# Moving slab transposes into the last stage, and opening the O*wo stage with the heads of wo that are there

## The chip, the cores and the metric

The kernel runs on one core of a Trainium2 chip. The metric is the time of one execution on the device, in microseconds (us). The core has five engines that run their own instruction streams: TensorE (PE, matrix products; its weight loads are shown as PEld), VectorE (DVE), ScalarE (ACT), GpSimd (POOL) and SyncE (SP). Here POOL and SP mostly issue DMAs: POOL plain copies, SP transposing ones. Each engine works in its own order and waits for the others by semaphores.

## The reference

The kernel computes a forward pass and its gradients. With x of 2048 x 576, 32 heads of width 128, keys and values given, and F = 4608:

```python
xn = layernorm(x)
q = heads(xn @ wq)
p = softmax(q @ k^T * Dh ** -0.5)
o = p @ v                      # rows of 32 * 128 columns
s = o @ wo
g = silu((sigmoid(xn @ w_gate) * (xn @ w_up)) @ w_down)
out = x + s * g
```

The outputs are `out` and the gradients of x, the keys, the values, wq, wo, w_gate, w_up and w_down for a given gradient of `out`. All arrays are bf16.

## The kernel before

The work runs in six stages, one after the other. Rows come in 16 tiles of 128 (NT = 16).

1. Layer norm, gate and up products; the activations go to DRAM.
2. The product with w_down, and everything that follows from it by rows. `g2_d` and `dsg_d` in DRAM keep the factors for the later O*wo stage.
3. Attention, one head after the other, forward and backward. Each head leaves its output columns in `on2_d`, its query gradient in `dq2_d` and two slabs in `kvT_d`: its key and value gradients, each 128 x 2048, still transposed. The stage exists twice in the program, as `attention(True)` and `attention(False)`; a flag computed on the device chooses one, and a branch leads around the other.
4. The O*wo stage (from L910): for each row tile, 32 heads x 2 products of `o` with wo (512 and 64 columns) into two accumulators, then ACT and DVE make `out` and the gradient `doB` of the inner product, which PE also transposes.
5. The gradients of the gated unit (b1, from L1034), 18 blocks of 256 columns.
6. The gradients of wo and wq (dwo and dwq, from L1126), 32 heads x 2 products, and last (from L1159) the gradient of x, in 8 pairs of row tiles. In the tables below these two parts are listed apart: the dwo and dwq stage and the last stage.

The parts that matter for the change:

**wo in old buffers.** wo is not given memory of its own. `wo_parts` places its 32 heads in buffers that attention stops using: heads 0 to 16 in `dsT` (dead 0), 17 to 19 in an old key buffer (dead 1), 20 to 22 in `Vn` (dead 2), 23 to 25 in `dOn` (dead 3) and 26 to 31 in the end of `xnT` (dead 4). While the last head is worked on, `paced` (L838) issues the loads, at most two heads each: a one-element POOL copy that waits for a slab of probabilities, then the DMA on POOL.

**The transposed output.** The O*wo stage needs each row tile of `on2_d` transposed: 128 x 4096, by one transposing DMA on SP (`load_oT`, L585). Three buffers `oTs` take turns: the memory of `KQ`, the end of `xnT`, and `xn_all`. Tiles 0 and 1 are loaded inside attention, tile 2 at the start of the O*wo stage, each later one when the tile three before it has been multiplied.

**Orders.** In stages 4 to 6 SP and POOL follow the order of the program text (`manual_schedule`), while the other engines are scheduled by dependences. In attention all are.

**Slabs.** The 64 slabs of `kvT_d` have to be turned (2048 rows of 128) and written to the outputs of the keys and values. `kv_turn` (L1018) issues the transposing DMA on SP into a tile `kvn` of two buffers; `kv_store` (L1025) issues the store on POOL, which waits for the transpose. Stage b1 does two of them for each of its 18 blocks. The dwo and dwq stage does one for each head until none is left.

**dwo and dwq.** For each head, `accumulate` (L978) runs 16 row tiles x 2 matmuls into one of four pairs of accumulators, and ACT copies the result out: to `dwo` (two buffers; stored by POOL, L1143) and to `dqT` (two buffers; turned by SP, L1145). Every eight heads POOL loads two blocks of 2 MB for the next eight (L1010, L1013). SP also loads w_up and w_gate transposed (L63).

**The last stage.** `seq` lists 80 chunks: for each pair of row tiles six chunks of 12 x 256 x 128 (from `du_d` and `dg_d`) and four of 8 x 256 x 128 (from `dq2_d`); the first two pairs are interleaved, so that their query chunks are numbers 12 to 19. SP loads each transposed (`load_chunk`, L1119) into one of four buffers (`ah`, `cf`), and PE multiplies it (L1188). SP loads wq transposed among chunks 3 to 11. When a pair is complete, `finish` (L1193) runs a chain on ACT and DVE and POOL stores two row tiles (L1218).

Of the kernel before, what the change touches and what calls it, by code (L numbers as in the profile page):

```python
# [13 lines left out]
P = 128  # L14
# [52 lines left out]
def kernel(  # L67
# [517 lines left out]
    def load_oT(dst, st):  # L585
        nc.sync.dma_start_transpose(dst, on2_d[st * P:(st + 1) * P, :])
# [8 lines left out]
    def attention(fast):  # L595
        with ExitStack() as es:
# [169 lines left out]
            def put(slot, cols, fn):  # L766
                units.setdefault(slot, []).append((cols, fn))
# [73 lines left out]
                load_wo_rows(view, view_h0[id(view)], a, b)  # L841
            view_h0 = {}
            for view, h0, n, dead in sorted(wo_parts, key=lambda w: dead_from[w[3]]):
                view_h0[id(view)] = h0
                for k in range(0, n, 2):
                    at = min([f for f in free if f >= dead_from[dead]] or [NT - 1])
                    if at in free:
                        free.remove(at)
                    put(bl + at, 0, lambda at=at, view=view, k=k, n=n: paced(at, view, k, min(k + 2, n)))
            for st in range(min(2, NT)):  # L850
                put(bl + NT + skew * st, 0, lambda st=st: load_oT(oTs[st], st))
            slot = 0
            while slot < 2 * NT * H or units:
                us = units.pop(slot, [])
# [19 lines left out]
    def late(name, bufs=1, **kw):  # L874
        return tc.tile_pool(name=name, bufs=bufs, reuse_waits="tile", **kw)
# [9 lines left out]
    with late("pc") as pc, late("pcw") as pcw, late("pcf") as pcf, \  # L885
# [22 lines left out]
                    nc.gpsimd.memset(wdT_sb[:LO, i, r0:r0 + WCH], 0.0)  # L908

        with late("c1l3", 4) as ldp3, late("c1s", 2) as sb, \  # L910
                late("c1ps", 2, space=PSUM) as ps, late("c1pt", 2, space=PSUM) as pst:
            wo_of = {}
            for view, h0, n, _ in wo_parts:
                for k in range(n):
                    wo_of[h0 + k] = view[:, k, :]
            oTs.append(oT_view(xn_all[:].rearrange("p t d -> p (t d)"), 0))
            if NT > 2:
                load_oT(oTs[2], 2)
            SG1 = 1
            NG1 = NT // SG1  # L920

            def group_loads(g):
                res = []
                for nm, src in (("dsg", dsg_d), ("g2b", g2_d), ("xb", x2)):
                    t_ = ldp3.tile([P, SG1, D], bf, name=nm)
                    nc.gpsimd.dma_start(t_[:], src[g * SG1 * P:(g + 1) * SG1 * P, :].rearrange("(t p) d -> p t d", p=P))
                    res.append(t_)
                return res

            groups = {g: group_loads(g) for g in range(min(2, NG1))}  # L930
            pend_tr = []
            for st in range(NT):
                if st and st + 2 < NT:
                    load_oT(oTs[(st + 2) % 3], st + 2)
                g, sl = divmod(st, SG1)
                if sl == 0:
                    if g + 2 < NG1:
                        groups[g + 2] = group_loads(g + 2)
                    dsg, g2b, xb = groups.pop(g)
# [8 lines left out]
                oT = oTs[st % 3]  # L948
                accs = [ps.tile([P, 512], f32, name=f"acc{j}") for j in range(len(ncs))]
                for h in range(H):  # L950
                    for j, (n0, nn) in enumerate(ncs):
                        nc.tensor.matmul(accs[j][:, :nn], lhsT=oT[:, h, :], rhs=wo_of[h][:, n0:n0 + nn],  # L952
                                         start=(h == 0), stop=(h == H - 1))
                s_sb = sb.tile([P, D], f32, name="s_sb")
                for j, (n0, nn) in enumerate(ncs):
                    alt.copy(s_sb[:, n0:n0 + nn], accs[j][:, :nn], eng="s")
                nc.vector.tensor_tensor(doB[:, st, :], s_sb[:], dsg[:, sl, :], op=ALU.mult)
                t0 = sb.tile([P, D], f32, name="t0")
                nc.vector.tensor_tensor(t0[:], s_sb[:], g2b[:, sl, :], op=ALU.mult)
                nc.vector.tensor_tensor(xb[:, sl, :], t0[:], xb[:, sl, :], op=ALU.add)  # L960
                if sl == SG1 - 1:
                    nc.gpsimd.dma_start(o0[g * SG1 * P:(g + 1) * SG1 * P, :].rearrange("(t p) d -> p t d", p=P), xb[:])
                pend_tr.append(st)
# [54 lines left out]
        def kv_turn(pool):  # L1018
            if kv_left:
                h, k = kv_left.pop(0)  # L1020
                t_ = pool.tile([P, NT, P], bf, name="kvn", bufs=2)
                nc.sync.dma_start_transpose(t_[:], kvT_d[h, k])
                kv_wait.append((t_, (out_2, out_3)[k][0, h]))

        def kv_store():  # L1025
            if kv_wait:
                t_, dst = kv_wait.pop(0)
                nc.gpsimd.dma_start(dst.rearrange("(p t) d -> p t d", t=NT), t_[:])
# [97 lines left out]
        with late("c2w") as wp, late("c2b") as blk, late("c2s", 2) as sb, late("c2ps", 4, space=PSUM) as ps:  # L1126
            dqTs = padded(wp, 2, "dqT")
            onqs = [(onb0, dqb0), tuple(blk.tile([P, NT, HG * P], bf, name=nm)[:] for nm in ("onb", "dqb"))]
            gap = max(1, (H - HG) // len(wT_pieces))
            for hg in range(NHG):  # L1130
                cols = slice(hg * HG * P, (hg + 1) * HG * P)
                onb, dqb = onqs[hg % 2]
                if hg + 1 < NHG:
                    load_on(onqs[(hg + 1) % 2][0], hg + 1)
                    load_dq(onqs[(hg + 1) % 2][1], hg + 1)
                dwq = dwqs[hg % 2]
                for hl in range(HG):
# [95 lines left out]
        pc3.release()  # L1233


# [28 lines left out]
```

## Time and profile before

| what | us |
|---|---|
| median of 4 runs | 5071.68 |
| lowest and highest of the 4 | 5055.66, 5083.19 |
| the profiled execution | 5058.23 |
| its span, first to last instruction | 5056.4 |
| attention ends, O*wo stage starts (first L952 matmul) | 3542.65 |
| dwo and dwq stage starts | 4297.70 |
| last stage starts | 4629.15 |
| attention starts (first score product, L638) | 483.4 |

The page shows PE busy for 97% of the span, DVE 50%, ACT 49%, POOL 18%. Busy time of PE is from modelled ends of matmuls, so a stage with PE busy all the time is not necessarily at the array's peak. A "share" of DMA is the time that packets took on the core's 16 DMA engines; where packets of two queues overlap it can pass 1. In the timeline, "SPq" and "POOLq" rows are the time an engine's queue spends on issuing a DMA; the brackets give the idle time before an instruction and what released it.

### The profile page before, as it was taken

How to read it: one execution, taken by the hardware profiler on the slowest of the kernel's cores; microseconds unless marked ns; L12 is line 12 of the kernel's file. 1: busy time of each engine (PE TensorE's matmuls, PEld its weight loads, DVE VectorE, ACT ScalarE, POOL GpSimd, SP SyncE). 2: the span in 40 equal slices, each digit the busy share in tenths (PEclk: the TensorE clock that was granted, in tenths of full speed). 3: DMA queues.
4: the chain of work that ended last, by engine and by line, in shares of the span. 5: the costliest groups of instructions: out<-in, count | busy, mean ns of one | idle time of the engine just before them, and what ended most of it. 6: DMA issues, size and time to landing. Idle time of an engine off the chain costs nothing.

```text
span 5056.4 us, 102037 instructions
## 1 busy us (share of the span) xinstructions
PE 4897.4 (97%) x41029; PEld 2902.2 (57%) x41029; DVE 2532.4 (50%) x6625; ACT 2501.7 (49%) x4576; POOL 887.9 (18%) x1379
## 2 busy tenths in 40 slices
PE   9999999999999999999999999999999899878999
PEld 4445666666666666666666666665456565434554
DVE  4544665665665665665665665665244443000111
ACT  4422766666666666666766766765123233111000
POOL 3322111111111111111111111111223222111000
PEclk9999999999999999999999999999999999989999
DMA  7887999999999999999999999999899999999976
GB/s 259 273 204 170 229 222 223 232 235 218 231 232 216 226 233 227 233 226 218 232 225 224 229 237 219 228 231 233 208 217 251 225 249 272 273 243 241 173 140 120
DMA packets 3053831, 1134.86 MB, mean 224 GB/s; under 512 B 2948321, under 2 KB 2952546, under 8 KB 3053346
## 3 DMA queue, kind: packets, MB, share of 16 engines
q1 hardware_dynamic: 2944738, 771.06, 83.5%
q0 software_dynamic: 108000, 356.60, 22.7%
q8 instruction: 322, 5.28, 0.4%
q14 instruction: 163, 1.34, 0.1%
q10 hardware_dynamic: 608, 0.59, 0.0%
HBM read 175.31 MB, written 215.68 MB: 77 GB/s over the span
## 4 chain that ended last, share of the span: by engine, by line
PE 85%; DMA 8%; issue 2%; SPq 2%; DVE 2%; ACT 0%; POOL 0%; POOLq 0%; ACTq 0%; DVEq 0%
PE acc L685 18%; PE acc L746 16%; PE sp L638 8%; PE dp L708 8%; PE acc L982 8%; PE acc L1188 6%; PE acc L217 5%; PE u_ps L452 3%; PE g_ps L450 3%; PE acc L535 3%; PE dh L1059 2%; PE acc L952 2%; DMA kvn<-kvT_d 2%; DMA out_dram<-dwo 1%; PE acct L147 1%
## 5 line engine op out<-in xcount | busy, mean ns | idle before, releaser
L656 ACT ACTIVATE Pq<-sp 128x1024 bf16<-128x1024 f32 x1024 | 1047.0, 1023 | 273.6 <-PE sp L638 264.2
L711 DVE SCALAR_TENSOR_TENSOR Pq<-dp,negdelta,Pq 128x1024 bf16<-128x1024 f32 x512 | 655.2, 1280 | 44.7 <-PE dp L708 44.7
L714 ACT ACTIVATE t<-dp,negdelta 128x1024 bf16<-128x1024 f32 x512 | 567.2, 1114 | 215.6 <-PE dp L708 201.1
L708 PE MATMUL dp<-VT,dOT 128*128 128x512 bf16 x2048 | 610.5, 380 | 2.3
L638 PE MATMUL sp<-KQ 128*128 128x512 bf16 x2048 | 609.3, 379 | 2.2 <-ACT Pq L656 2.1
L685 PEld LDWEIGHTS <-dST 128*128 128x128 bf16 x8192 | 508.4, 98 | 150.4 <-DMA dST<-Pq 8.4
L685 PEld LDWEIGHTS <-PT 128*128 128x128 bf16 x8192 | 501.9, 98 | 141.6 <-DMA PT<-Pq 22.4
L685 PE MATMUL acc<-Kn,dST 128*128 128x128 bf16 x8192 | 557.0, 219 | 5.7 <-DMA dST<-Pq 5.6
L685 PE MATMUL acc<-Vn,PT 128*128 128x128 bf16 x8192 | 544.6, 220 | 15.6 <-DMA PT<-Pq 15.5
L746 PE MATMUL acc<-Pq,dOn 128*128 128x512 bf16 x2048 | 531.9, 379 | 0.0
L746 PE MATMUL acc<-Pq,Qn 128*128 128x512 bf16 x2048 | 526.7, 380 | 0.0
L715 DVE TENSOR_TENSOR Pq<-t,Pq 128x1024 bf16<-128x1024 bf16 x512 | 354.4, 692 | 318.3 <-ACT t L714 307.2
L1205 DVE SCALAR_TENSOR_TENSOR junk<-acc,xn_all 128x512 f32<-128x512 f32 (+1 forms) x32 | 13.9, 453 | 722.7 <-ACT dxn L1204 722.7
L726 ACT ACTIVATE dq_n<-acc,rsc 128x128 bf16<-128x128 f32 x512 | 187.5, 366 | 331.9 <-PE acc L685 310.5
L746 PEld LDWEIGHTS <-Qn 128*128 128x128 bf16 x2048 | 200.4, 98 | 240.9 <-issue 1.6
L746 PEld LDWEIGHTS <-dOn 128*128 128x128 bf16 x2048 | 199.1, 98 | 234.8 <-issue 1.6
L708 PEld LDWEIGHTS <-dOT 128*128 128x128 bf16 x2048 | 179.0, 98 | 124.6 <-issue 12.6
L638 PEld LDWEIGHTS <-KQ 128*128 128x128 bf16 x2048 | 179.1, 98 | 123.7 <-issue 3.1
L679 POOL DMA_DIRECT2D on_d<-o_n x128 | 97.1, 759 | 789.2 <-DVE junk L697 458.7
L643 DVE TENSOR_REDUCE rs_all<-rsp 128x1 f32<-128x2 f32 x512 | 78.4, 153 | 305.9 <-ACT Pq L656 294.3
L679 POOL DMA_DIRECT2D dq_d<-dq_n x128 | 98.0, 765 | 705.9 <-ACT dq_n L726 666.1
L1060 DVE SCALAR_TENSOR_TENSOR nbl<-ah 128x256 bf16<-128x256 bf16 x288 | 98.8, 420 | 244.1 <-DMA ah<-h_d 235.0
(210 smaller groups left out, 6737.8 us busy)
## 6 DMA issues: line engine op xcount, KB each, us to landing
out_dram<-kvn POOLq DMA_DIRECT2D x64, 512.0 KB, 8.8
ah<-a_d POOLq DMA_DIRECT2D x18, 1024.0 KB, 12.3
ah<-h_d POOLq DMA_DIRECT2D x18, 1024.0 KB, 14.7
du_d<-du_blk POOLq DMA_DIRECT2D x18, 1024.0 KB, 15.9
dg_d<-dg_blk POOLq DMA_DIRECT2D x18, 1024.0 KB, 17.9
h_d<-h_row POOLq DMA_DIRECT2D x64, 256.0 KB, 3.5
a_d<-a_row POOLq DMA_DIRECT2D x64, 256.0 KB, 3.8
x_all<-in_A_k_cache_dram SPq DMA_DIRECT2D x64, 256.0 KB, 3.8
```

The lines of the kernel that those rows point to most:

```text
L217: nc.tensor.matmul(av[:, :CH], lhsT=w[:, i, :], rhs=srcT[:, i, cs], start=(i == 0), stop=(i == DT - 1))
L638: nc.tensor.matmul(sp[:, c * CH:(c + 1) * CH], lhsT=hs.QT[:, qt * P:(qt + 1) * P], rhs=hs.KT[:, hf * HW_ + c * CH: hf * HW_ + (c + 1) * CH ...
L656: nc.scalar.activation(Pq[:, hsl], sp[:], AF.Exp, scale=SCALE, accum_out=hs.rsp[:, hf:hf + 1])
L679: nc.gpsimd.dma_start(dst_d[q0 * P:(qt + 1) * P, hs.h * P:(hs.h + 1) * P].rearrange("(t p) d -> p t d", p=P), buf[:])
L685: nc.tensor.matmul(hs.acc[:, 0, :], lhsT=T[:, kt, :], rhs=rhs[:, kt, :], start=(kt == 0), stop=(kt == NT - 1))
L708: nc.tensor.matmul(dp[:, c * CH:(c + 1) * CH], lhsT=hs.dOT[:, qt * P:(qt + 1) * P], rhs=hs.VT[:, hf * HW_ + c * CH: hf * HW_ + (c + 1) * C ...
L711: nc.vector.scalar_tensor_tensor(Pq[:, hsl], dp[:], hs.negdelta[:, qt:qt + 1], Pq[:, hsl], op0=ALU.add, op1=ALU.mult)
L714: nc.scalar.activation(t[:], dp[:], AF.Identity, bias=hs.negdelta[:, qt:qt + 1], scale=1.0)
L715: nc.vector.tensor_tensor(Pq[:, hsl], t[:], Pq[:, hsl], op=ALU.mult)
L746: nc.tensor.matmul(self.acc, lhsT=self.nat[:, qt, :], rhs=self.slabs[qt][:, cs], start=(qt == self.lo), stop=(qt == self.hi - 1))
L982: nc.tensor.matmul(accs[j][:, :nn], lhsT=lhs[:, st, cols], rhs=rhs[:, st, n0:n0 + nn], start=(st == 0), stop=(st == NT - 1))
L1188: nc.tensor.matmul(self.accs[sl][j][:, :nn], lhsT=ch[:, kk, sl * P:(sl + 1) * P], rhs=wT[:, k0 + kk, n0:n0 + nn], start=(self.k + kk == 0) ...
```

## The change

Three things are changed.

- The nine heads of wo in the three dead buffers 1, 2 and 3 are no longer loaded during attention. Their loads, one for each buffer, are issued in the O*wo stage. Of the transposed outputs only tile 0 is loaded during attention; tiles 1 and 2 are loaded in the O*wo stage.
- The O*wo stage multiplies the 23 heads that are there (`h_early`) for tiles 0, 1 and 2, one after the other, and then the nine others (`h_late`) for each of the three. The other 13 tiles run over all heads, the early ones first. The accumulators have three buffers in place of two. What follows a tile's products is moved into `close`, with the loads for the tile three later; the row loads (`row_loads`) are three tiles ahead in place of two.
- The dwo and dwq stage turns no slabs. The slabs left over by stage b1 are turned in the last stage: from chunk 10 on, at every second chunk, `kv_store` for the slab before and `kv_turn` for the next (two `kvn` buffers in the stage's pool `chp`).

```diff
             for view, h0, n, dead in sorted(wo_parts, key=lambda w: dead_from[w[3]]):
+                if dead in (1, 2, 3):
+                    continue
                 view_h0[id(view)] = h0
...
-            for st in range(min(2, NT)):
-                put(bl + NT + skew * st, 0, lambda st=st: load_oT(oTs[st], st))
+            put(bl + NT, 0, lambda: load_oT(oTs[0], 0))
...
-                late("c1ps", 2, space=PSUM) as ps, late("c1pt", 2, space=PSUM) as pst:
+                late("c1ps", 3, space=PSUM) as ps, late("c1pt", 2, space=PSUM) as pst:
...
+            h_early = [h0 + k for _, h0, n, dead in wo_parts if dead not in (1, 2, 3) for k in range(n)]
+            h_late = [h0 + k for _, h0, n, dead in wo_parts if dead in (1, 2, 3) for k in range(n)]
             oTs.append(oT_view(xn_all[:].rearrange("p t d -> p (t d)"), 0))
-            if NT > 2:
-                load_oT(oTs[2], 2)
...
+            R0 = min(3, NT)
+            loads = {}
+            for st in range(1, R0):
+                load_oT(oTs[st], st)
+            loads[0] = row_loads(0)
+            for view, h0, n, dead in wo_parts:
+                if dead in (1, 2, 3):
+                    load_wo_rows(view, h0, 0, n)
+            for st in range(1, R0):
+                loads[st] = row_loads(st)
...
+            def mm(st, hs_):
+                if st not in accs_of:
+                    accs_of[st] = [ps.tile([P, 512], f32, name=f"acc{j}") for j in range(len(ncs))]
+                oT = oTs[st % 3]
+                for h in hs_:
+                    for j, (n0, nn) in enumerate(ncs):
+                        nc.tensor.matmul(accs_of[st][j][:, :nn], lhsT=oT[:, h, :], rhs=wo_of[h][:, n0:n0 + nn],
+                                         start=(h == h_early[0]), stop=(h == (h_early + h_late)[-1]))
+
+            def close(st):
+                accs = accs_of.pop(st)
+                dsg, g2b, xb = loads.pop(st)
+                if st + R0 < NT:
+                    load_oT(oTs[st % 3], st + R0)
+                    loads[st + R0] = row_loads(st + R0)
...
+            for st in range(R0):
+                mm(st, h_early)
             for st in range(NT):
...
+                mm(st, h_late if st < R0 else h_early + h_late)
+                close(st)
...
                     lcols = slice(hl * P, (hl + 1) * P)
-                    kv_turn(blk)
                     dwo = sb.tile([P, D], bf, name="dwo")
...
                     nc.sync.dma_start_transpose(dwq[:, :, lcols], dqTs[h % 2][:])
-                    kv_store()
...
-            while kv_left or kv_wait:
-                kv_turn(blk)
-                kv_store()
...
                 if n not in chunks:
                     chunks[n] = load_chunk(n)
+                if n >= len(seq) // 8 and n % 2 == 0:
+                    for _ in range(-(-len(kv_left) // max(1, (len(seq) * 7 // 8 - n) // 2))):
+                        kv_store()
+                        kv_turn(chp)
...
                 row_of[sbi].mul(chunks.pop(n), wT, k0, which[2])
+                if not kv_left:
+                    kv_store()
+            while kv_left or kv_wait:
+                kv_turn(chp)
+                kv_store()
```

More of the change, by code (lines that the diff above doesn't have):

```diff
@@ L915, with row_loads @@
                     wo_of[h0 + k] = view[:, k, :]
+            h_early = [h0 + k for _, h0, n, dead in wo_parts if dead not in (1, 2, 3) for k in range(n)]
+            h_late = [h0 + k for _, h0, n, dead in wo_parts if dead in (1, 2, 3) for k in range(n)]
             oTs.append(oT_view(xn_all[:].rearrange("p t d -> p (t d)"), 0))
-            if NT > 2:
-                load_oT(oTs[2], 2)
-            SG1 = 1
-            NG1 = NT // SG1
-            def group_loads(g):
+            def row_loads(st):
@@ L923, in group_loads @@
                 res = []
                 for nm, src in (("dsg", dsg_d), ("g2b", g2_d), ("xb", x2)):
-                    t_ = ldp3.tile([P, SG1, D], bf, name=nm)
-                    nc.gpsimd.dma_start(t_[:], src[g * SG1 * P:(g + 1) * SG1 * P, :].rearrange("(t p) d -> p t d", p=P))
+                    t_ = ldp3.tile([P, D], bf, name=nm)
+                    nc.gpsimd.dma_start(t_[:], src[st * P:(st + 1) * P, :])
                     res.append(t_)
                 return res
-            groups = {g: group_loads(g) for g in range(min(2, NG1))}
@@ L931 @@
-            pend_tr = []
-            for st in range(NT):
[L933 to L939, printed above, removed]
+            R0 = min(3, NT)
+            loads = {}
+            for st in range(1, R0):
+                load_oT(oTs[st], st)
@@ new lines @@
+            loads[0] = row_loads(0)
[4 more added lines that the diff above has]
+                loads[st] = row_loads(st)
+            pend_tr = []
+            accs_of = {}
+            def mm(st, hs_):
[6 more added lines that the diff above has]
+                                         start=(h == h_early[0]), stop=(h == (h_early + h_late)[-1]))
@@ new lines, in close @@
+            def close(st):
[4 more added lines that the diff above has]
+                    loads[st + R0] = row_loads(st + R0)
+                s_sb = sb.tile([P, D], f32, name="s_sb")
+                for j, (n0, nn) in enumerate(ncs):
+                    alt.copy(s_sb[:, n0:n0 + nn], accs[j][:, :nn], eng="s")
+                nc.vector.tensor_tensor(doB[:, st, :], s_sb[:], dsg[:], op=ALU.mult)
+                t0 = sb.tile([P, D], f32, name="t0")
+                nc.vector.tensor_tensor(t0[:], s_sb[:], g2b[:], op=ALU.mult)
+                nc.vector.tensor_tensor(xb[:], t0[:], xb[:], op=ALU.add)
+                nc.gpsimd.dma_start(o0[st * P:(st + 1) * P, :], xb[:])
+                pend_tr.append(st)
@@ L947 @@
                     transpose_to(nc, pst, doB[:, st_, :], D, doBT, st_ * P, ident, alt, eng="s")
[L948 to L963, printed above, removed]
+                mm(st, h_late if st < R0 else h_early + h_late)
+                close(st)
             while len(wd_pieces) > (F // WCH - 1) * DT:
```

## The prediction

> **What bounds the kernel now.** I read the page first: TensorE (PE) is busy 97% of the 5056.4 us span, so only a stage where it is not can give much. Then the table of stages (columns: stage, length, busy time of PE, weight loads, DVE, ACT, POOL with instruction counts, granted clock, DMA share, GB/s):
>
> ```profile
> 308.00:3542.65 3234.65, 3206.56 (x28240) 1990.02 (x28237) 2020.99 (x5272) 2087.28 (x3576) 497.87 (x789) 1.00 1.13 225
> 3542.65:3695.00 152.35, 144.66 (x1190) 77.99 (x1191) 44.03 (x79) 24.34 (x58) 41.48 (x75) 0.97 0.86 201
> 3695.00:4297.70 602.70, 577.24 (x4813) 354.07 (x4811) 257.25 (x834) 181.68 (x495) 169.86 (x216) 0.98 1.09 247
> 4297.70:4629.15 331.45, 263.20 (x2048) 133.40 (x2049) 0.00 (x0) 42.99 (x126) 60.77 (x94) 0.90 1.09 262
> 4629.15:5056.40 427.25, 410.14 (x3330) 211.12 (x3328) 52.29 (x160) 14.97 (x66) 18.56 (x34) 0.99 0.81 149
> ```
>
> The fourth stage (dwo and dwq) stands out: PE works 263 of 331 us, at clock 0.90, while the DMA share is 1.09. The fifth (the last stage) is PE's own, with a DMA share of 0.81. The waits of the fourth stage say why:
>
> ```profile
> POOL out_dram L1028 <- DMA kvn<-kvT_d: 248.3, 28, 20.4
> ACT dwo L40 <- DMA out_dram<-dwo: 237.7, 27, 32.0
> PE acc L982 <- ACT dwo L40: 68.3, 7, 19.8
> ```
>
> Read from the bottom (us in total, times, longest): PE waits 68.3 us for ACT to empty an accumulator; ACT waits for a dwo store, since dwo has two buffers; the store is behind a slab's store on POOL, which waits for that slab's transpose (kvn<-kvT_d). The slabs are the cause, as queue traffic and as bytes.
>
> The O*wo stage starts with a stop (timeline: start, length, engine, line):
>
> ```profile
> 3542.65 2.61 PE L952 MATMUL acc<-dsT,KQ 128*128 128x512 bf16 x20 [1.13 <-issue]
> 3550.14 3.54 PE L952 MATMUL acc<-dsT,KQ 128*128 128x512 bf16 x14 [4.88 <-DMA kvT_d<-VT]
> 3550.54 0.55 POOL L926 DMA_DIRECT2D dsg<-dsg_d  x1 [7.37 <-issue]
> ```
>
> PE stops after 20 matmuls and POOL stops too, both for no named work; they resume 0.4 us apart. The named store (VT) is read by no matmul there. Just before, in attention's end, PE waits for transposes:
>
> ```profile
> PE acc L685 <- DMA PT<-Pq: 6.2, 2, 3.7
> PE acc L685 <- DMA dST<-Pq: 3.5, 1, 3.5
> ```
>
> **What the Trainium skill says.** (1) "Trainium Kernel Development and Optimization", Key Constraints: DMAs issued from SP, ACT and POOL run on the same 16 DMA engines and interleave. The trace agrees: in the fourth stage the two queues' shares add to 1.09. (2) "DMA: Bandwidth & Descriptors", Latency and other measured facts, gives 261 GB/s for a DMA transpose in one kernel. Here it is lower: from 4652.5 to 4705 SP issues transposes back to back and moves 11.13 MB, 212 GB/s, so 4.7 us per MB; I use that. (3) "Runtime: NRT & Kernel Launch", Instruction fetch mechanics: a taken branch whose target isn't loaded stalls the engine. That fits the 4.88 and 7.37 us just after the branch around the unused second attention; the change leaves the branch, so I leave the stop. (4) "TensorE: Matmul & The Clock Gate", Part 1: after idling, PE runs at half clock for about 3.4 us. The trace agrees: 14 matmuls took 3.54 us after the stop, 20 took 2.61 before.
>
> **The change, part by part** (against the profiled execution, 5058.23 us, 1.8 us of it outside the span).
>
> *Fourth stage, slabs removed.* 28 of the 64 slabs are turned there (28 waits above); 36 stay in the stage before it, unchanged. What is left for PE is 64 products (32 heads, dwo and dwq) of 32 matmuls; six take 23.52 us in the chain, so one 3.92 us and all 64 x 3.92 = 250.9 us. Is the DMA then still late? The stage moves 32.4 MB by transposes and 54.0 MB plain; a slab is 128x2048 bf16, 0.524 MB, turned and stored, so 14.7 MB leave each: 17.7 MB x 4.7 = 83 us, and 39.3 MB plain at 2.5 us per MB (an estimate: the busiest slices move 400 GB/s) = 98 us, together 181 of 251 us. PE binds. The next lateness is the 4.2 MB load of two blocks per eight heads, in front of dwo stores on the same ring: about 10 us, inside the slack of four accumulators (15.7 us). I leave 6 us of stalls: 257 us, a gain of 74. Bounds: 55 (a stall per block stays) and 80.
>
> *Last stage, slabs added.* One turn at each second chunk from 10 to 64. TensorE needs 50.96 us per pair of row tiles (ten chunks). DMA per pair now: six chunks of 0.786 MB and four of 0.524, 6.81 MB x 4.7 = 32 us; five slabs add 2.62 MB x 4.7 = 12.3 us, and their stores 2.62 x 2.5 = 6.6 us: 51 us. So the DMA becomes just as long as PE, with nothing to spare. Cheap bound: no cost from bytes. Dear bound: the trace puts the DMA share at 0.77 for what I price at 32 of 51 us (0.63); with that busy time, 106 us of added work (28 x 3.8) meet 0.23 x 280 = 64 us of room, and 42 us are exposed. I take 10.
>
> Queues: SP issues chunk loads and turns in one order, with four chunk buffers. A turn needs a slab buffer (two), freed by the store of two turns earlier on POOL. At the end of each pair of row tiles POOL's dx stores, which wait for the finishing chain, stand ahead of that store. In the trace the chain ends 6.1 us after PE's last matmul of the pair (4789.53 to the second dx store at 4795.59). So a turn comes about 6 us plus the store's 5.6 us (median to landing in the fourth stage) late, and the next chunk load behind it. That chunk is needed three chunks on: 3 x 3.92 = 11.8 us after the first pair (queries alone), 17.6 us later. Add 2.5 us for the turn and 4.5 for the landing: 18.7 us, so 7 us of stall at chunk 19 and 1 us at each of five later ends; with cold clock after them about 15 us in all. Bounds 0 and 25.
>
> What comes back: the last stage now starts with 5.2 us of waits for chunks (4.29, 0.72, 0.17) and a cold clock, since SP came late from the fourth stage's slabs. Chunks 0 and 1 will be there early, so -6. The sum of the last stage: 10 + 15 - 6, about +20 (bounds -3 and +55). The 11 us tail after the last matmul is unchanged; turns end 15 chunks ahead of it.
>
> *O*wo stage and attention's end.* Six loads for nine heads (1.33 MB) and six small POOL copies leave the last head's second half; the transpose of row tile 1 (5.06 us on SP, among attention's own) moves behind the branch. Each delays attention's transposes, whose PE waits (6.2 + 3.5, and about as much cold clock) can mostly go: gain 6, bounds 0 and 12. Behind the branch, transposes for tiles 1 and 2 run while PE stands in the fetch stop; three tiles x 23 heads x 2 matmuls (16.9 us when warm) then cover the three loads of 0.44 MB, issued about 3 us after POOL resumes. Same matmuls, same count. Late next: row tile 3 loads only when tile 0 closes, about 4.4 us of matmuls ahead of need, and its transpose takes 4.6 us plus landing: +2, bounds 0 and 6. The third accumulator buffer costs nothing. Together -4.
>
> Sum: -74 + 20 - 4 = -58 us: 5000 against the profiled execution. That one is low among the five times shown (mean 5068, median of four 5071.68), so for a typical run I say 5068 - 58 = 5010.
>
> **The rivals.**
> A (forecast): the fourth stage becomes PE's, the last stage gives back some 20 us. 5010, own range 4990 to 5032. Chance 0.65.
> B: the last stage becomes the DMA's, at the dear bound: +42 from bytes, +15 from queues, -6. Net -74 + 51 - 4 = -27: 5041, to 5060 if the fourth stage also keeps 20 us of stalls. For it: a DMA share of 1.08 at the start of this stage, where PE did wait. Against: attention lives with 1.13 and PE 99% busy. Chance 0.16.
> C: the last stage hides all (-3), attention's end gives 8: -85, 4983. For it: the lookahead of four chunks. Against: 51 of 51 us leaves no room. Chance 0.12.
> D (slower): the stall of the fourth stage moves whole. Place: SP in the last stage, where a turn held up by its store blocks the chunk loads. Price: the longest such wait now is 20.4 us; if each of 28 turns cost PE 3.8 us (that is 106 us), the stage loses 106 + 15 - 6 = 115 against 78 gained: +37, 5105. It decides from (78 - 9) / 28 = 2.5 us per turn. For it: the same POOL order did exactly this before. Against: here nothing PE needs soon waits behind the slab's store. Chance 0.05.
> E: the change doesn't do what it says: the block loads of 4.2 MB hold back the dwo stores as the slabs did, the fourth stage stays at 310 us, and -21 + 20 - 4 leaves 5063. Chance 0.02.
>
> **How the numbers follow.** The time is A's. What a measurement can tell from no change is about 0.5%, 25 us. Faster: A, C and 0.05 of B, 0.82. Within: the rest of B and E, 0.12. Slower: D and a remainder, 0.06. The range 4983 to 5047 takes in A, C's centre and most of B.
>
> **What would show it.** In the profile after: the fourth stage at 251 to 265 us, clock near 1.0, no kvn in it; the last stage at 435 to 455 us, its DMA share about 1.0, PE's waits there on cf and ah loads, first near chunk 19; PE still stopping after about 20 matmuls behind the branch; attention's PT and dST waits smaller. Wrong: a fourth stage over 290 us, or a last stage over 480.

## The result, and the profile after

The changed kernel takes 5044.51 us (median of 42 runs, 5007.07 to 5078.47), the kernel before 5066.58 in the same comparison (63 runs): ratio 0.9953, 95% interval 0.9938 to 0.9967, so 17 to 31 us gained where 58 were forecast. Ratios and ranges here and below leave out slow runs, those over 1.5% above the fastest of their kernel; medians are of all runs. The profiled execution took 5034.21 us (span 5032.4, clock 0.992) against 5058.23. The table of stages of the changed kernel (columns as in the table of the kernel before; stages from attention to the last):

```profile
308.00:3544.04 3236.04, 3206.52 (x28238) 1988.77 (x28237) 2021.07 (x5272) 2088.85 (x3576) 494.53 (x776) 1.00 1.14 224
3544.04:3685.90 141.86, 132.90 (x1099) 69.82 (x1100) 33.40 (x47) 19.52 (x47) 39.69 (x70) 0.98 0.91 213
3685.90:4320.58 634.68, 593.00 (x4902) 364.04 (x4901) 267.93 (x866) 187.08 (x507) 174.95 (x224) 0.97 1.09 239
4320.58:4571.47 250.89, 250.89 (x2049) 129.64 (x2050) 0.00 (x0) 43.35 (x126) 45.97 (x66) 1.00 0.84 230
4571.47:5032.40 460.93, 415.26 (x3330) 210.76 (x3328) 52.29 (x160) 14.99 (x66) 33.67 (x62) 0.97 1.00 202
```

The fourth row is exactly what the forecast asked for: 250.89 us, PE busy in all of it, clock 1.00. The last stage is 461 us in place of 427 at a DMA share of 1.00. The third row is the surprise: stage b1 (the gradients of the gated unit), whose code isn't touched, takes 634.7 us. (The table of before divided the two stages at 3695; divided at the first `dh` matmul, 3683.77, as here, its b1 was 613.9 and its O*wo stage 141.1.)

| profiled executions | before | after | difference | forecast |
|---|---|---|---|---|
| attention's end (start of O*wo) | 3542.65 | 3544.04 | +1.4 | -6 |
| O*wo stage | 141.1 | 141.9 | +0.7 | +2 |
| stage b1 | 613.9 | 634.7 | +20.8 | none |
| dwo and dwq stage | 331.5 | 250.9 | -80.6 | -74 |
| last stage | 427.2 | 460.9 | +33.7 | +20 |

The waits of the changed kernel in the last stage (us in total, times, longest):

```profile
PE acc L1199 <- DMA cf<-dq_d: 10.8, 5, 5.5
...
PE acc L1199 <- DMA cf<-dg_d: 7.0, 6, 1.7
PE acc L1199 <- DMA cf<-du_d: 6.3, 1, 6.3
...
SPq L1038 <- DMA out_dram<-kvn: 27.5, 6, 5.6
```

PE now waits for chunks, 32 us with the `ah` chunks, and SP waits six times for a slab's store before it can turn the next. The longest wait of the first line stands at chunk 19, where the forecast put it. This looked like the forecast queue hold-ups; the experiments say otherwise.

At the start of b1, the timeline (start, length, engine, line) of before and then of after shows a different spacing between a slab's turn on SP and the load of `xn_all` on POOL:

```profile
3686.60 2.07 SPq L1022 DMA_TRANSPOSE kvn<-kvT_d  x1
...
3688.05 1.17 POOL L1041 DMA_DIRECT2D xn_all<-xn_d  x1
```

```profile
3689.42 2.48 SPq L1038 DMA_TRANSPOSE kvn<-kvT_d  x1
3689.61 1.18 POOL L1057 DMA_DIRECT2D xn_all<-xn_d  x1
```

Before, the turn is issued 1.45 us ahead of the load, after, 0.19 us. The load (2.36 MB) lands in 11.3 us before and in 20.6 after, and PE waits 6.4 us for it. Measured from the first `dh` matmul, the turn comes 0.7 us later than before and the load 0.6 us earlier. The load's landing before, after, and in a later run that moves this turn away:

```profile
xn_all<-xn_d POOLq DMA_DIRECT2D x1, 2304.0 KB, 11.3
```

```profile
xn_all<-xn_d POOLq DMA_DIRECT2D x1, 2304.0 KB, 20.6
```

```profile
xn_all<-xn_d POOLq DMA_DIRECT2D x1, 2304.0 KB, 10.6
```

### The profile page after: what moved, and what is told of

Its sections match the earlier page's. It is cut to its first block, busy times and chain, and to the rows that moved or that the text cites. A ratio compares the mean times of both kernels' runs of the same rounds, so it can differ in the third digit from the quotient of the medians.

```text
span 5032.4 us, 102041 instructions
## 1 busy us (share of the span) xinstructions
PE 4894.9 (97%) x41029; PEld 2898.9 (58%) x41029; DVE 2532.5 (50%) x6625; ACT 2504.3 (50%) x4576; POOL 888.5 (18%) x1370
## 4 chain that ended last, share of the span: by engine, by line
PE 86%; DMA 8%; issue 2%; DVE 2%; SPq 1%; ACT 0%; POOL 0%; POOLq 0%; DVEq 0%; ACTq 0%
PE acc L685 18%; PE acc L746 16%; PE acc L998 10%; PE sp L638 9%; PE dp L708 8%; PE acc L217 5%; PE acc L1199 4%; PE u_ps L452 3%; PE g_ps L450 3%; PE acc L535 3%; DMA ah<-h_d 3%; PE acc L948 2%; PE dh L1075 2%; DMA PT<-Pq 1%; PE acct L147 1%
## 5 line engine op out<-in xcount | busy, mean ns | idle before, releaser
L685 PEld LDWEIGHTS <-PT 128*128 128x128 bf16 x8192 | 501.3, 98 | 144.1 <-DMA PT<-Pq 24.4
L1215 ACT ACTIVATE dxn<-acc 128x512 f32<-128x512 f32 (+1 forms) x32 | 12.8, 407 | 433.5 <-PE acc L1199 426.0
```

Of the source, the lines that this page charges most:

```text
L685: nc.tensor.matmul(hs.acc[:, 0, :], lhsT=T[:, kt, :], rhs=rhs[:, kt, :], start=(kt == 0), stop=(kt == NT - 1))
```

## The experiments

All stage lengths come from one profiled execution each; totals are ratios to the kernel before, run beside it on the same chip. Two theories opened: the loss in b1 belongs to the O*wo part of the change (theory 1), or it is chance (theory 2).

**Only the slabs.** The kernel before with `kv_turn` and `kv_store` moved as in the change, nothing else.

> The kernel before with only the 28 slabs moved from the dwo/dwq stage to the last stage; the O*wo stage stays as before. Theory 1 (the 20.7 us that stage b1 lost come from the O*wo part of the change, which brings b1's first transposes and loads to another moment): b1 stays near 614 us, dwo/dwq stage 251, last stage 455 to 461, total 45 us under before, ratio 0.991. Theory 2 (b1's loss is the chance of one profiled execution, or comes with any move, and the slabs' gain is smaller than the stage table says): ratio 0.995 to 0.996, like the whole change. As forecast for this part (-74 + 20): ratio 0.989.

Ratio 0.9923, interval 0.9888 to 0.9958 (median 5028.9): 39 us gained, by the middle of the interval more than by the whole change, though the two intervals overlap. The stages b1, dwo/dwq and last:

```profile
3688.89:4309.16 620.27, 581.31 (x4832) 361.06 (x4902) 268.27 (x867) 187.15 (x508) 175.69 (x226) 0.98 1.09 246
4309.16:4562.40 253.24, 250.94 (x2007) 130.15 (x2049) 0.00 (x0) 43.23 (x126) 44.54 (x64) 0.99 0.86 224
4562.40:5027.10 464.70, 414.26 (x3263) 212.23 (x3328) 52.38 (x160) 14.97 (x66) 33.57 (x62) 0.97 1.00 200
```

b1 is near its old length, the last stage as long as with the whole change. The interval alone would not exclude theory 2.

**Only the O*wo part.** The changed kernel with the slabs put back into the dwo/dwq stage.

> The kernel before with only the O*wo part of the change (three row tiles over the early heads, nine heads of wo loaded then, third accumulator buffer); slabs stay in the dwo/dwq stage. Theory 1: this part costs about 20 us, in b1, first block about 42 us and later blocks of 39 to 45 us: ratio 1.004. Theory 2: ratio 1.000 within 0.0015, b1 614 to 620 us. As forecast (-4): ratio 0.999.

Ratio 1.0018, interval 0.9999 to 1.0037: this part costs 0 to 19 us, where the forecast had a gain of 4. b1 took 648.0 us, `xn_all` landed in 28.3 us and PE waited 14.2 us for it. So a loss in b1 comes with this part.

**No slabs in the last stage.** 28 head rows of the key and value gradients are left out.

> The changed kernel without the 28 slabs at all: they are turned neither in the dwo/dwq stage nor in the last stage, so 28 of the 64 head rows of two outputs are not written. What the slabs cost in the last stage shows as the difference to the changed kernel. If the 33.7 us that the last stage gained in length are the slabs' own: last stage 421 to 428 us and a total 34 to 40 us under the changed kernel (ratio to before 0.988). Rival (the last stage's start stalls 6.3 + 0.5 + 1.3 + 0.4 us are of another cause, the chunk loads that are queued behind the last dwq transposes): about 8 us of stall stay at the first chunks, last stage 430 to 435.

Ratio 0.9862, interval 0.9822 to 0.9903 (median 4991.85). The last stage:

```profile
4545.42:4973.90 428.48, 406.55 (x3263) 210.88 (x3328) 52.28 (x160) 14.98 (x66) 18.57 (x34) 0.98 0.80 148
```

So the slabs cost this stage about 32 us. A stall of 6.0 us at chunk 3 stays without any slab: as the rival said, that start stall has another cause. It comes in some executions and not in others (6.3 us in the changed kernel, none with only the O*wo part), so a few us between two of these stages can be its doing.

**Which half of a slab costs: queue or bytes?** Theory Q puts the cost on hold-ups in the queues, theory B on full DMA engines. Two kernels take one half of each slab away from the changed kernel: turns whose results are not stored (28 head rows left out), and stores of other data without turns (those rows hold other numbers). The first:

```diff
-                        kv_store()
+                        kv_wait.clear()
                         kv_turn(chp)
...
```

> The changed kernel with the 28 turns of the last stage but without the 28 stores (those 28 head rows of two outputs are not written). No turn then waits for a store. Theory Q (hold-ups behind POOL's stores, 15 us in the forecast, 27.5 us of SP waits in the trace): the waits of turns go, the 5.5 us stall at chunk 19 goes, last stage about 440, total 15 to 20 us under the changed kernel. Theory B (the transpose ring is full: 92% of 290 us by transposes alone): last stage 450 to 460, total 0 to 10 us under the changed kernel.

> The changed kernel with 28 plain stores of 0.524 MB in the last stage, at the same chunks, but no turns (they store other data, so those head rows are wrong). Theory B (the transposes fill the DMA): last stage 425 to 432, total about 45 us under the changed kernel, close to the kernel without slabs. Theory Q or one in which all bytes count alike: last stage 440 to 450.

Their last stages, turns first:

```profile
4560.21:4986.50 426.29, 405.81 (x3263) 210.37 (x3328) 52.25 (x160) 15.00 (x66) 18.59 (x34) 0.99 0.96 184
```

```profile
4589.76:5032.90 443.14, 409.16 (x3263) 211.84 (x3328) 52.27 (x160) 14.99 (x66) 50.93 (x62) 0.97 0.94 177
```

Turns alone cost nothing that shows, though they bring the DMA share to 0.96 (ratio 0.9874, interval 0.9842 to 0.9906; the start stall is not in this execution). Stores alone cost about 15 us (ratio 0.9866, interval 0.9829 to 0.9904), which is high for two reasons: the stored rows were read in pieces of 256 bytes, unlike a slab's, and POOL, with no turn to wait for, issued the stores in bursts of up to five within some 5 us. PE's two long waits, 6.6 and 10.0 us, come just behind such bursts. Theory B as stated (the transposes fill the DMA) failed in both. Theory Q did better, but turns without stores also lack the stores' bytes, and came out 14 us below its number. The next kernel is to separate waits from bytes.

**Same bytes, no dependency.** Turns and stores as in the changed kernel, but each store reads a weight that is there already (those head rows hold other numbers): no turn waits for a store, no store for a turn.

```diff
-                        kv_store()
+                        if kv_wait:
+                            nc.gpsimd.dma_start(kv_wait.pop(0)[1].rearrange("(p t) d -> p t d", t=NT), junk_sb)
                         kv_turn(chp)
...
```

> The changed kernel with the same 28 turns and 28 stores in the last stage, at the same chunks and of the same bytes, but the stores read other data (a weight that is already there), so no turn waits for a store and no store for a turn; those head rows of two outputs are wrong. Theory Q (the wait of a turn for its buffer's store, in SP's one order, is what costs): last stage 426 to 435, as with turns alone. Theory B (the bytes together fill the DMA): last stage 450 to 461. Between, both count.

```profile
4568.22:5036.10 467.88, 416.38 (x3263) 212.87 (x3328) 52.30 (x160) 15.00 (x66) 33.52 (x62) 0.96 1.01 199
```

467.9 us: without any hold-up between turns and stores the stage is as long as with them (ratio 0.9940, interval 0.9913 to 0.9966; median 5048.26 beside 5069.10). Alone this doesn't settle theory Q, since here too the stores leave in bursts of four or five, and PE's longest wait, 11.4 us, follows one. Two complete kernels do. Four slab buffers (two of them in memory that the dwq blocks have left, for the stage's pool has no room for four):

```diff
-                        kv_store()
-                        kv_turn(chp)
+                        if len(kv_wait) > 1:
+                            kv_store()
+                        kv_turn4()
...
```

> The changed kernel, complete, with four slab buffers in the last stage (two new ones in memory that the dwq blocks have left) and each store issued one turn later. If Theory Q holds: no SP wait of a turn for a store, last stage 426 to 438, total 22 to 34 us under the changed kernel (ratio to before 0.990). If Theory B: last stage 450 to 461.

SP's 27.5 us of waits are gone, the last stage takes 458.2 us (DMA share 1.03), ratio 0.9940, interval 0.9910 to 0.9970; some stores leave in bursts. And the stores ahead of the dx stores, where they leave one by one:

```diff
-                        kv_store()
                         kv_turn(chp)
+                elif n % 2:
+                    kv_store()
```

> The changed kernel, complete, two slab buffers, with each slab's store issued one chunk after its turn, in front of the finishing chain's dx stores in place of behind them. My forecast's own hold-up (stores behind dx stores at the five pair ends, 15 us) as the cause: the 5.5 us stall at chunk 19 goes, last stage 440 to 448. If every store's landing counts, not only those at pair ends, or if bytes count: last stage 452 to 461.

```profile
4595.84:5056.60 460.76, 413.28 (x3263) 211.31 (x3328) 52.29 (x160) 14.97 (x66) 33.58 (x62) 0.98 1.04 202
```

460.8 us, no SP wait for a slab's store either; the stall near chunk 19 shrinks to 2.5 us, but others take its place (4.4 us at 4825). Ratio 0.9923, interval 0.9894 to 0.9953, a total that can't be told from the changed kernel's (median 5055.11 beside 5069.10). Theory Q falls: by these profiles the hold-ups cost at most some 5 us. What costs is turns and stores together. In all eight profiles with 28 of each in the last stage, those below included, it takes 454 to 468 us and moves 199 to 205 GB/s, in whatever order; turns alone still fit.

**The collision at the start of b1.** The changed kernel with the second turn of the first block moved:

```diff
                 kv_store()
-                kv_turn(ldp)
+                if fb:
+                    kv_turn(ldp)
...
+                    if fb == 0 and nm == "dwg":
+                        kv_turn(ldp)
                     stg_ = outp.tile([P, DT, FB], bf, name=nm)
...
+                if fb == 0:
+                    kv_store()
```

> The changed kernel with one edit in stage b1: the second slab turn of the first block is issued after the dwu transposes, no longer beside the 2.36 MB load of xn_all. Theory C (the O*wo part moved that turn from 1.5 us ahead of the load to 0.2 us beside it, and the two slow each other: 20.6 us to landing in place of 11.3): no PE wait for xn_all, first block 34 us in place of 42 to 50, total 8 to 12 us under the changed kernel. Rival (the load is late because of the load of the next block or earlier stores): xn_all still lands after 18 to 25 us, total unchanged.

`xn_all` landed in 10.6 us, PE didn't wait for it, and the first block took 33.5 us in place of 42.1. (Ratio 0.9894, interval 0.9852 to 0.9937, too wide to size 8 us.) The other profiles with this order agree. By how much the turn is issued ahead of the load, and the load's time to landing, in us:

| O*wo stage | gap, landing |
|---|---|
| old | 1.28, 11.3; 1.37, 11.3; 1.45, 11.3; 1.48, 11.2; 1.50, 11.1; 1.76, 10.7; 1.77, 10.7 |
| changed | -0.17, 28.3; -0.10, 28.3; -0.07, 24.6; 0.00, 28.6; 0.19, 20.6; 0.35, 24.4; 0.36, 12.0; 0.37, 20.4 |

With 1.3 us or more between them they don't disturb each other; within 0.4 us the load takes up to 2.6 times as long. The gap alone doesn't decide it (0.35 and 0.36 us gave 24.4 and 12.0). Within each row the kernels differ only in stages after b1.

**The middle of b1: chance or not?** In the profiled execution of the last kernel (one of the two slowest of its six runs) b1 was still 656.4 us long, by waits for the next block's `ah` loads. So the first block is not all. The kernel before, profiled twice more:

> The kernel before, profiled again. Theory M (the changed O*wo stage also causes the waits in the middle of b1): waits for ah loads after the first block of 14 to 29 us, as in the four profiles with the old O*wo stage. Theory N (those waits are chance, the same for both): a value anywhere from 3 to 57 us, over 30 as likely as not. In both: gap between turn and xn_all load about 1.5 us, landing 11 us, attention's end at 3540 to 3552 us.

> The kernel before, profiled once more, to the same question and with the same expectations: theory M 14 to 29 us of waits for ah loads after b1's first block, theory N anywhere from 3 to 57 us.

b1 took 602.9 and 617.3 us, and PE waited 0.8 and 16.3 us after the first block: the first fits neither theory M (14 to 29) nor N (3 to 57), so these two decide nothing. Two candidates with the old O*wo stage gave two more profiles, one with the four buffers, one with the slabs shared between the stages (14 turned at every second head of the dwo/dwq stage, stored two heads later; 14 in the last stage):

> The candidate to beat both: slabs in the last stage with four buffers, O*wo stage as in the kernel before. If Theory Q holds and the O*wo part costs 8 to 12 us by itself: dwo/dwq stage 251 to 253, last stage 426 to 438, first block of b1 34 us, total 68 to 75 us under the kernel before, ratio 0.986. If Theory B: like the slabs-only version, 0.992.

> The kernel before with the slabs shared: 14 turned in the dwo/dwq stage, one each second head, each stored two heads after its turn so that POOL never waits for a turn, and 14 in the last stage, one each fourth chunk; O*wo stage as before. Theory: 14 slabs of 3.8 us of DMA fit into the 70 us of room of the dwo/dwq stage (251 to 256 us) and the last stage falls to 432 to 440: total 60 to 70 us under the kernel before, ratio 0.987, 25 us under the slabs-only version. Rival (bytes in the dwo/dwq stage hold back dwo's stores again, whatever the order on POOL): dwo/dwq stage over 270, no gain over slabs-only.

Four buffers: ratio 0.9925, interval 0.9893 to 0.9956, last stage 454.5 us, b1 634.8. Shared: 0.9867, interval 0.9834 to 0.9899, the dwo/dwq stage 279.7 us (worse than expected, its dwo stores wait again) but the last stage 430.4, b1 616.6. A sharing of 9 and 19 came next, with the old and with the changed O*wo stage (in the latter with the first block's turn moved; its edit against the changed kernel is shown, without that move):

```diff
+                    if h % 3 == 2 and h < 27:
+                        kv_store()
+                        kv_turn(blk)
...
-                if n >= len(seq) // 8 and n % 2 == 0:
+                if n >= len(seq) // 8 and n % 3 == 0:
...
```

> O*wo stage as before, slabs shared 9 to 19: nine turned in the dwo/dwq stage (one each third head, stored three heads later), 19 in the last stage (one each third chunk). The last stage cost 3 to 9 us with 14 slabs and 34 to 38 with 28, the dwo/dwq stage 27 with 14: with 9 and 19 I expect dwo/dwq 255 to 265, last stage 432 to 445, total 60 to 75 us under the kernel before, ratio 0.986, at or a little under the 14 and 14 version.

> The same sharing, with the changed O*wo stage and b1's second turn moved away from the xn_all load. If the O*wo part gains at attention's end (9 us in the mean of the profiles) and nothing else is against it: 5 to 10 us under the version with the old O*wo stage. If theory M holds (13 us more in the middle of b1): equal or up to 5 us over it.

Ratios 0.9857 (0.9822 to 0.9892) and 0.9881 (0.9852 to 0.9909); dwo/dwq 254.6 and 256.7 us, last stage 432.2 and 426.9. The last stage of the second:

```profile
4576.25:5003.20 426.95, 410.04 (x3330) 210.95 (x3328) 52.29 (x160) 14.98 (x66) 29.26 (x54) 0.98 1.03 197
```

So a DMA share of 1.00 isn't by itself the limit: with 19 slabs the share is 1.03 and the stage costs nothing more than without slabs. The version with the changed O*wo stage is not ahead, though it leaves attention earlier: its b1 took 644.5 us against 606.1. Over all profiles so far b1 is 616.0 us in the mean of seven with the old O*wo stage (602.9 to 634.8) and 643.0 in ten with the changed one (619.5 to 670.8), so on average it does belong to the change, though single executions overlap. The first block makes 9 of these 27 us (34.0 to 42.6 in the means), PE's waits behind it 18 (15.6 to 33.4). At b1's end PE also waits for the first block of `on_d`, 13 us with the old stage and 9 with the changed one. In b1 of the kernel before and then of the changed kernel the waits read:

```profile
DVE nbl L1060 <- DMA ah<-h_d: 235.0, 17, 31.7
...
POOL out_dram L1028 <- DMA kvn<-kvT_d: 190.1, 15, 25.6
```

```profile
DVE nbl L1076 <- DMA ah<-h_d: 257.6, 17, 27.6
...
POOL out_dram L1044 <- DMA kvn<-kvT_d: 157.9, 12, 22.9
```

POOL stands up to 22.9 us for a slab's turn, and stood up to 25.6 us before, so this wait isn't new with the change. The next loads of `ah` are behind it, and go out late and beside further turns. If that is the cause, moving the second turn behind the dwu transposes in *all* blocks should empty the middle of b1:

```diff
                 kv_store()
-                kv_turn(ldp)
...
+                    if nm == "dwg":
+                        kv_turn(ldp)
                     stg_ = outp.tile([P, DT, FB], bf, name=nm)
...
+                kv_store()
```

> The 9 and 19 sharing with the old O*wo stage, and in all blocks of b1 the second slab turn issued after the dwu transposes. Theory C in general (a turn issued beside a 1 MB plain load makes both late, and that is what stops the middle of b1): waits for ah after the first block near 0 to 5 us, b1 about 600 us, total 5 to 15 us under the same kernel without this edit (ratio to before 0.984). Rival (b1 is simply full of bytes, DMA share 1.09): waits of 8 to 29 us stay, total the same or worse.

> The same with the changed O*wo stage. Theory C in general: waits for ah near 0 to 5 us too, b1 about 600 us in place of 644, total 20 to 35 us under the version with only the first turn moved, and level with or below the one with the old O*wo stage. Rival: waits of 20 to 57 us stay.

Ratios 0.9799 (0.9765 to 0.9833, median 4958.91) and 0.9794 (0.9760 to 0.9828, median 4960.04): 100 us under the kernel before, and the O*wo parts are level. By the ratios the edit gains 29 us with the old O*wo stage and 44 with the changed one, more than the 5 to 15 and 20 to 35 expected. The stages b1, dwo/dwq and last with the changed O*wo stage:

```profile
3677.90:4261.53 583.63, 581.49 (x4901) 359.31 (x4900) 267.95 (x866) 187.28 (x507) 173.97 (x223) 1.00 0.95 259
4261.53:4522.69 261.16, 254.55 (x2049) 130.94 (x2049) 0.00 (x0) 43.09 (x126) 50.75 (x75) 0.99 1.01 257
4522.69:4952.60 429.91, 410.04 (x3330) 210.44 (x3328) 52.29 (x160) 15.00 (x66) 29.26 (x54) 0.99 1.00 196
```

b1 is PE's alone, 583.6 us, less than in any profile without this edit. Last, the changed kernel with this one edit:

> The changed kernel with one edit: in every block of b1 the second slab turn is issued after the dwu transposes. If b1's collisions were the missing term of the forecast: b1 600 to 605 us, last stage still 455 to 468, total 30 to 45 us under the changed kernel (ratio to before 0.987 to 0.989). If the last stage were the larger part: under 15 us.

Ratio 0.9853, interval 0.9835 to 0.9871 (median 4978.6): by the difference of the ratios, 0.0100, some 51 us under the changed kernel, by the medians 66, more than the 30 to 45 expected. Its stages from O*wo to the last:

```profile
3530.23:3670.78 140.55, 132.69 (x1099) 69.76 (x1100) 33.45 (x48) 19.52 (x47) 39.57 (x70) 0.98 0.92 215
3670.78:4254.44 583.66, 581.50 (x4902) 359.47 (x4901) 267.77 (x866) 187.30 (x507) 173.94 (x223) 1.00 0.95 259
4254.44:4505.32 250.88, 250.88 (x2048) 129.03 (x2049) 0.00 (x0) 43.27 (x126) 46.40 (x67) 1.00 0.89 232
4505.32:4969.90 464.58, 419.13 (x3330) 211.83 (x3328) 52.27 (x160) 15.00 (x66) 33.55 (x62) 0.97 1.01 200
```

Of the stages only b1 has changed against the changed kernel, by 51 us (attention ends 14 us earlier, which lies within its scatter over the twelve profiles with this O*wo stage, 3528.9 to 3544.5). PE's waits for `ah` are gone, POOL waits for no slab's turn, and DVE's longest wait for `ah` is 12.5 us in place of 27.6. The DMA view of b1 shows how; the changed kernel first, then with the edit (queue: packets, MB, share; then issues: count, size, median us to landing):

```profile
q1 hardware_dynamic: 141393, 35.15, 50.7%
...
ah<-h_d POOLq DMA_DIRECT2D x17, 1024.0 KB, 16.7
...
kvn<-kvT_d SPq DMA_TRANSPOSE x36, 7.6
```

```profile
q1 hardware_dynamic: 139249, 34.61, 38.3%
...
ah<-h_d POOLq DMA_DIRECT2D x17, 1024.0 KB, 11.5
...
kvn<-kvT_d SPq DMA_TRANSPOSE x36, 4.9
```

The same 35 MB of transposes take 51% of the engines' time in the changed kernel, and 38% of a shorter stage with the edit: 322 us against 224. The edit takes away two things at once, the meeting and POOL's wait for the turn ahead of the loads; only the first block shows the meeting alone. How much of the middle of b1 each makes wasn't tried, nor why the middle suffers more behind the changed O*wo stage than behind the old one.

## Why the prediction was right or wrong

The direction was right; the size was wrong by more than half: -22 us measured (interval -17 to -31), -58 forecast. The means over all profiles give each term with less scatter than the two first executions, though over different kernels and chips:

| term | forecast | measured, means of profiles |
|---|---|---|
| dwo/dwq stage | -74 | -78 (329.9 in four with all slabs there, 252.1 in eleven with none) |
| last stage | +20 | +37 (426.3 in four with its slabs in the stage before, 463.5 in four with 28 and the changed kernel's scheme) |
| attention's end | -6 | -11 (3546.8 in eight, 3535.7 in twelve) |
| O*wo stage | +2 | +1 (139.9 in eight, 140.9 in twelve) |
| stage b1 | none | +27 (616.0 in seven, 643.0 in ten) |
| sum | -58 | -24 |

**dwo/dwq stage: right**, with its mechanism. 64 products of 3.92 us are 250.9 us, and 250.89 came out. The 6 us left for stalls were not needed, and no `kvn` is left in the stage. Its DMA sum was low (0.84 of 251 us is 211, where 181 was forecast), which did no harm here and did in the last stage. (The plain bytes were read as 54.0 MB; the view has 54.27.)

**Attention's end and the O*wo stage: right in the mean**, though the first profile seemed to deny it. PE's waits for the transposes `PT` and `dST` in the last 110 us of attention fell from 16.3 us in the mean to 9.1, and PE waits 2.7 to 3.8 us for row tile 3, both as forecast. PE does stop behind the branch as before (5.1 us).

**The step that failed most is a term put at nothing: stage b1.** The prediction dismisses it with "36 stay in the stage before it, unchanged". It looked at SP and POOL up to the O*wo stage's end and took b1 as unchanged because its code and its slabs are. The runs show +27 us there. But the change moves SP's slab turn and POOL's load of `xn_all` against each other by 1.3 us, from 1.45 us apart to 0.19. In seven of eight profiles this costs 8 to 16 us in the first block, by a collision that moving the turn removes. The rest lies in the middle, and why the change makes it worse stays open; that the order of the second turn removes all of it is shown. The prediction's own table had hints: a DMA share of 1.09 in b1, and a b1 that was not PE's own (577 of 603 us busy). That the stage held 30 us of loss before, all of it removable by the order of one transpose and its store, I had not seen at all.

**The last stage: right in kind, too small.** The cause that was named for most of the +20, queue hold-ups (+15), is not it: with the stores ahead of the dx stores SP waits for none of them, and the stage is no shorter. The term for bytes (+10) was mis-sized: with the hold-ups at most some 5 us, bytes make nearly all of the +37. Two views of before disagreed, my price (0.63 of the time busy) and the trace's share (0.77), and I took the price, which had left out 5.3 MB of plain traffic (0.07 of the share). The share was the truer account of the engines' time: 0.80 of 428 us without slabs is 343 us of DMA time; with turns 0.96 of 426, 409 us. A turn thus cost 2.4 us of DMA time, as priced (2.5). If the stage with the stores as well counts as full, 1.00 of 461 us, a slab's store took (461 - 409) / 28 = 1.9 us, where 0.524 MB at 2.5 us per MB had given 1.3. The "dear bound", +42 from bytes, came close in part by luck: the 0.77 is the share from 4705 to 5045, and in the 280 us where the turns were to run (4690 to 4970) it was 0.84, which gives 106 - 0.16 x 280 = 61. So the price was too low and the share, read over the right stretch, too high.

The start stalls, "-6", came back in some executions only, and not by the cause named: 6.0 us are there even without slabs.

**Against the rivals.** The changed kernel landed nearest to rival B (5041, the last stage the DMA's), by two causes of which B had one. Its total is near by luck: B has +51 in the last stage, where +37 was measured, and nothing in b1, where +27 was. The last stage's 461 us lie just above the 435 to 455 that the forecast wanted to see. D's mechanism, SP blocked by slabs' stores, is what the kernels with four buffers and with the stores ahead refute.

The Trainium skill's sentence that DMAs from different queues interleave on the same 16 engines ("Trainium Kernel Development and Optimization", Key Constraints) fits the trace: in b1 of the changed kernel the two queues' shares add to 1.08. But the interleaving is not free here: the first block's load takes 20 to 29 us beside a turn in seven of eight profiles, against 11.

## What to carry to other kernels

When DMAs are moved, check every later stage in which a big plain transfer and a transposing one are issued close together, also where the code is unchanged: here a shift of 1.3 us decided whether they met. For the cost of filling a stage take two bounds: here a sum of bytes by prices gave too little (10 us), and the DMA share over the stretch to be filled too much (61), where about 35 came. A share of 1.00 isn't where the room ends: 28 slabs and 19 both brought it there, and only the 28 cost time. Keep what fills it spread: here 9 slabs in one stage and 19 in the other cost little where 28 in either cost 37 to 78 us. A transpose that nothing waits for did best behind the urgent loads, not beside them, with its store not ahead of the next urgent load on its queue.

## What was unexpected in the hardware

- A transposing DMA of 0.5 MB and a plain load of 2.36 MB issued within 0.4 us of each other: the load landed in 12.0 to 28.6 us, in seven of eight cases over 20, against 10.7 to 11.3 with 1.3 us or more between them. The turn suffers too: up to 25.5 us to landing in place of 5.0 to 5.6.
- Turns alone raised the last stage's DMA share from 0.80 to 0.96 without costing PE anything that shows; stores on top cost about 35 us. Yet 19 turns with their stores ran at shares of 1.00 to 1.03 in 427 to 432 us. Full with 28, the stage moved 199 to 205 GB/s, while b1 with the late turns moves 259: no one rate is the limit for every mix of transfers.
- The best versions ranged over 4952 to 4971 us in six runs and 4945 to 4965, where the kernel before ranged over 5042 to 5090 beside them. But beside the last experiment nine runs of it lay within 5046 to 5061, so whether such meetings make its spread stays open.
